# Windowed attention and a gated convolution on one core: second scores moved behind the values, on three single banks

## The chip, the cores and the metric

The kernel runs on one core of a Trainium2 chip. What counts is the device time of one execution in microseconds; the shown time is the median of three runs. The engines are TensorE (PE, with its weight loads as PEld), VectorE (DVE), ScalarE (ACT), GpSimd (POOL) and SyncE (SP), which issues the transfers. Each works through its own instructions in the order in which they were issued.

## The reference, cut to what matters

```python
# attention: q, k, v are [4, 8, 768, 64] fp32; n_sink = 4, window = 128
scores = q @ k.T / 8                       # per batch and head
keep   = (key < n_sink) | (0 <= query - key < window)
a = softmax(where(keep, scores, -1e9))     # denominator + 1e-9
x = a @ v                                  # then [4, 768, 512]
# gated convolution, d_model = 512, 5 taps, along the sequence
gate = sigmoid(causal_conv(x, conv_w))
out  = (gate * (x @ w_val)) @ w_out
```

Each query looks at 128 keys behind it and at the four sink keys; the first queries of a sequence have no keys of an earlier block.

## The kernel before

The work is cut into 24 *steps*: four batches, three blocks p of 256 rows, two groups qd of four heads. Two steps make a *module* of 256 rows by 512 channels. A step loads its q, k and v. `scores` (L343 on) is called twice, for two heads each (s0 and s1): eight small 64x64 fp32 matmuls (L356; the trace shows each as two) write 200 columns for each of two halves c and two heads j into `ss`, a tile of two PSUM banks that exists once. DVE then moves the diagonal block (copy_predicated, L361) and masks and takes the minimum of each half (L366). ACT takes exponentials (L374), DVE the reciprocal (`recip`, L379 and L380), POOL normalises (L388) and makes the sinks' shares. PE transposes the probabilities in two groups of four (L405, `probs_t`: tx and ty) into `tr`, a pool of two banks; `probs_x` on DVE (L427, L429) and `probs_y` on ACT (L436) spread them into the masked weights `wt`. PE transposes the sinks (L410), DVE masks them (L420). `values` (L453) makes xv from `wt` and v with 64x64 matmuls, `sinks` (L460) adds to it with 128-wide ones. ACT copies xv (`xt` L470, `xh` L474, and the four columns of the past, L478), POOL makes the low part `xl` (L484) and the last tap (L488), DVE the other four taps in eight instructions (L496), ACT the tanh (L501). A module then has four `val` calls (L515, 12 matmuls each; v0 to v3), `gated` on DVE (L526), its high part on ACT (L530) and its low part on POOL (L534), four `outp` calls (L545, 6 matmuls each; o0 to o3), and two stores (L549 on ACT, L551 the transfer). High and low parts take three passes of fp32r matmuls instead of one in fp32.

The order is written by hand: tables give each call of each step a time, in steps, and all calls are issued sorted by it. `WHEN` holds the general times, `EARLY` the exceptions of the first and last steps, `DECODE` those of the weights, which arrive as float64 bits and are decoded at the start (`_decode`; `bias` is L146 and L166). `FIRST` and `FILL` give idle matmuls at the start (`busy`, L219). The four calls on one bank line:

```python
ps_s = ctx.enter_context(tc.tile_pool(name="ps_s", bufs=1, space=PSUM))   # ss: one tile of two banks
ps_t = ctx.enter_context(tc.tile_pool(name="ps_t", bufs=2, space=PSUM))   # tr: two tiles of one bank
```

In `WHEN`, s0 is at -0.1928 and s1 at 0.3255, values at 1.8427, counted from the start of the own step; so s0 of a step stands just before the values of the step two earlier, and s1 about half a step behind them.

Of the kernel before, what the change touches and what calls it, by code (L numbers as in the profile page):

```python
# [19 lines left out]
DM = 512  # L20
# [14 lines left out]
WHEN = dict(kq=-1.9615, vv=-0.3611, s0=-0.1928, e0=0.4814, s1=0.3255, e1=0.5848, rec=0.6245, vl=1.4302, norm=0.667,  # L35
            tx=0.9562, ty=1.2383, sk=1.1919, ev=1.1901, yv=1.3942, ts=1.226, val=1.8427, si=1.874, xc=2.044,
            xh=2.2668, hd=2.0069, xl=2.2917, c4=2.0938, c0=2.2838, c1=2.5363, th=2.774, v0=0.4208, v1=0.4433,
            v2=0.7542, g0=0.6699, v3=0.8679, h0=0.7252, l0=1.0416, g1=0.9504, h1=1.0551, l1=1.282, o0=1.3729,
            o1=1.5265, o2=1.3969, t0=2.127, o3=2.081, t1=2.5321, cw=-67.148)

EARLY = {("kq", 0): -111.3041, ("vv", 0): -51.6322, ("s0", 0): -67.4875, ("e0", 0): -63.9472, ("s1", 0): -63.8218,
# [52 lines left out]
        ("scores", (3, 0)): 10}  # L94
SKA = 6

CUT = [("wo", 0), ("wo", 1), ("wo", 2), ("wo", 3)]
LAG = 3


# [30 lines left out]
def _decode(nc, pool, raw, n, whi, wlo, shape, unit=None, bank=None):  # L131
# [29 lines left out]
    def high():  # L161
        nc.scalar.activation(out=whi, in_=tf, func=AF.Copy)
# [635 lines left out]
```

## Time and profile before

| what | us |
|---|---|
| median of three runs | 282.35 |
| the three runs | 281.14, 282.35, 282.41 |
| the profiled execution, its time | 280.02 |
| its span, first to last instruction | 278.1 |
| PE busy | 264.1 |
| DVE busy | 221.5 |
| ACT busy | 180.8 |
| POOL busy | 175.6 |

The mean granted TensorE clock over the span was 0.993 of full speed. Busy times are sums over instructions that partly overlap, so an engine's share near 100% says that it hardly waited, and a pitch (start to start) says what one instruction costs the queue.

### The profile page before, as it was taken

How to read it: one execution, taken by the hardware profiler on the slowest of the kernel's cores; microseconds unless marked ns; L12 is line 12 of the kernel's file. 1: busy time of each engine (PE TensorE's matmuls, PEld its weight loads, DVE VectorE, ACT ScalarE, POOL GpSimd, SP SyncE). 2: the span in 40 equal slices, each digit the busy share in tenths (PEclk: the TensorE clock that was granted, in tenths of full speed). 3: DMA queues.
4: the chain of work that ended last, by engine and by line, in shares of the span. 5: the costliest groups of instructions: out<-in, count | busy, mean ns of one | idle time of the engine just before them, and what ended most of it. 6: DMA issues, size and time to landing. Idle time of an engine off the chain costs nothing.

```text
span 278.1 us, 8153 instructions
## 1 busy us (share of the span) xinstructions
PE 264.1 (95%) x2981; PEld 215.1 (77%) x2984; DVE 221.5 (80%) x827; ACT 180.8 (65%) x605; POOL 175.6 (63%) x226
## 2 busy tenths in 40 slices
PE   8897699999999999999999999999999999999991
PEld 3444369679789789789788888888888798798880
DVE  5999999988977986986986896896887898877510
ACT  3799967846865874774785685675676668564421
POOL 3378976974875675566667748648658729647330
PEclk9999999999999999999999999999999999999997
DMA  6993960047516417318317326336236232010202
GB/s 198 328 377 123 354 192 13 1 144 247 154 42 202 147 40 242 106 42 245 106 44 245 100 87 204 101 113 180 96 116 202 76 128 59 11 67 2 75 5 85
DMA packets 27391, 36.87 MB, mean 133 GB/s; under 512 B 2256, under 2 KB 23760, under 8 KB 27344
## 3 DMA queue, kind: packets, MB, share of 16 engines
q1 hardware_dynamic: 27344, 36.27, 40.1%
q8 instruction: 26, 0.43, 0.6%
q14 instruction: 21, 0.17, 0.2%
HBM read 29.97 MB, written 6.29 MB: 130 GB/s over the span
## 4 chain that ended last, share of the span: by engine, by line
PE 77%; POOL 8%; DVE 6%; ACT 5%; issue 2%; POOLq 0%; ACTq 0%
PE acc L515 23%; PE acc L545 21%; PE ss L356 11%; PE xv L453 10%; PE tr L405 6%; PE acc L219 3%; PE xv L460 3%; POOL wx L388 2%; DVE sg L496 2%; ACT w L374 2%; DVE sx L366 1%; POOL sg L488 1%; ACT xt L470 1%; POOL xl L484 1%; POOL wol L178 1%
## 5 line engine op out<-in xcount | busy, mean ns | idle before, releaser
L388 POOL TENSOR_TENSOR wx<-w,sm 128x512 f32<-128x512 f32 x48 | 49.3, 1047 | 60.2 <-DVE sm L380 45.2
L496 DVE SCALAR_TENSOR_TENSOR sg<-xv,cw,sg 128x256 f32<-128x256 f32 x192 | 78.9, 475 | 5.8 <-POOL sg L488 5.8
L374 ACT ACTIVATE w<-sx,ngm 128x132 f32<-128x132 f32 x192 | 75.1, 398 | 4.1 <-DVE ngm L366 4.1
L515 PE MATMUL acc<-xh,wvh 128*128 128x256 f32 x192 | 49.3, 291 | 0.3 <-ACT xh L474 0.3
L515 PE MATMUL acc<-xh,wvl 128*128 128x256 f32 x192 | 47.1, 280 | 0.0
L366 DVE CUSTOM_DVE_ANT_0 sx<-ss,mask 128x132 f32<-128x132 f32 x192 | 45.2, 292 | 1.6
L356 PE MATMUL ss<-k,q 64*64 64x200 f32 x768 | 43.6, 342 | 1.7 <-DVE ngm L366 0.8
L545 PE MATMUL acc<-woh,gh 128*128 128x512 f32 x96 | 39.9, 416 | 0.0
L515 PEld LDWEIGHTS acc<-xh,wvh 128*128 128x128 f32 x192 | 36.0, 188 | 3.9 <-DVE sg L496 2.3
L545 PE MATMUL acc<-woh,gl 128*128 128x512 f32 x96 | 38.1, 397 | 0.0
L545 PE MATMUL acc<-wol,gh 128*128 128x512 f32 x96 | 38.0, 396 | 0.1
L374 ACT ACTIVATION_READ_ACCUMULATOR w<-sx,ngm 128x1 f32 x192 | 37.1, 193 | 0.0
L515 PEld LDWEIGHTS acc<-xh,wvl 128*128 128x128 f32 x192 | 36.2, 189 | 0.0
L356 PEld LDWEIGHTS ss<-k,q 64*64 64x64 f32 x768 | 24.9, 132 | 14.3 <-issue 8.7
L534 POOL TENSOR_TENSOR gl<-sg,gh 128x512 fp32r<-128x512 f32 x24 | 31.5, 1313 | 5.7 <-ACT gh L530 5.7
L453 PEld LDWEIGHTS xv<-wt,v 64*64 64x64 f32 x1024 | 32.2, 133 | 3.4 <-ACT wt L436 0.9
L453 PE MATMUL xv<-wt,v 64*64 64x192 f32 (+2 forms) x1024 | 33.5, 274 | 0.4 <-ACT wt L436 0.4
L484 POOL TENSOR_TENSOR xl<-xt,xh 128x512 fp32r<-128x512 f32 x24 | 30.9, 1288 | 1.7 <-ACT xh L474 1.7
L515 PE MATMUL acc<-xl,wvh 128*128 128x256 f32 x192 | 30.8, 281 | 0.9 <-POOL xl L484 0.9
L488 POOL TENSOR_TENSOR sg<-xt,cw 128x512 f32<-128x512 f32 x24 | 25.2, 1051 | 10.2 <-ACT xt L470 10.1
L405 PE MATMUL tr<-ident,wx 128*128 128x128 f32 x192 | 28.2, 274 | 0.0
L361 DVE COPY_PREDICATED ss<-low,ss 128x256 f32<-128x256 uint8 x48 | 20.3, 424 | 9.2 <-PE ss L356 9.0
(108 smaller groups left out, 426.5 us busy)
## 6 DMA issues: line engine op xcount, KB each, us to landing
k<-in_kt_dram SPq DMA_DIRECT2D x23, 408.0 KB, 4.1
v<-in_vt_dram SPq DMA_DIRECT2D x16, 384.0 KB, 3.4
out_dram<-osb SPq DMA_DIRECT2D x24, 256.0 KB, 2.1
q<-in_qt_dram SPq DMA_DIRECT2D x23, 256.0 KB, 4.3
raw<-in_w_val_dram SPq DMA_DIRECT2D x4, 512.0 KB, 6.1
v<-in_vt_dram SPq DMA_DIRECT2D x8, 256.0 KB, 3.6
raw<-in_w_out_dram SPq DMA_DIRECT2D x4, 512.0 KB, 6.1
vs<-in_vsk_dram SPq DMA_DIRECT2D x8, 128.0 KB, 3.5
```

The costliest lines, as they stand in the source:

```text
L356: nc.tensor.matmul(ss[e * D:(e + 1) * D, j, c * n:(c + 1) * n], q[js, g, (2 * c + e) * D:(2 * c + e + 1) * D], k[js, g, (2 * c + e) * HB:( ...
L366: nc.vector.tensor_tensor_reduce(out=sx[:, j, c], in0=sv[:, j, c, :PK], in1=mask[:, c if p == 0 else 2], op0=ALU.add, op1=ALU.min, scale=- ...
L374: nc.scalar.activation(out=w[:, g, j, c], in_=sx[:, j, c], func=AF.Exp, scale=-1.0, bias=ngm[:, g, j, c:c + 1], accum_out=sm[:, g, j, c:c ...
L388: nc.gpsimd.tensor_tensor(out=t[:, n].rearrange("p c h x -> p h c x"), in0=w[:, :, :, at], in1=sm.to_broadcast([P, 4, 2, D]), op=ALU.mult)
L405: nc.tensor.transpose(out=x[:, o:o + P], identity=ident, in_=ws[s][:, n, c, 2 * g:2 * g + 2].rearrange("p j x -> p (j x)"))
L453: nc.tensor.matmul(acc[o * D:(o + 1) * D, g, x0 + h * D:x0 + (h + a1 - a0 + 1) * D], v[js, g, n], t[js, g, n, a0:a1 + 1].rearrange("p a r ...
L484: nc.gpsimd.tensor_tensor(out=xl[:, g], in0=xts[s], in1=xh[:, g].bitcast(F32), op=ALU.subtract)
L488: nc.gpsimd.tensor_tensor(out=sg[s // 2][:, g], in0=xts[s], op=ALU.mult, in1=cw[:, g, KT - 1:].to_broadcast([P, 2, PQ]))
L496: nc.vector.scalar_tensor_tensor(out=g, in0=x, scalar=a, in1=g, op0=ALU.mult, op1=ALU.add)
L515: nc.tensor.matmul(acc[:, h], a[:, kc, cs], x[:, kc], start=(n == 0), stop=(n == 11))
L534: nc.gpsimd.tensor_tensor(out=gl, in0=g, in1=gh.bitcast(F32), op=ALU.subtract)
L545: nc.tensor.matmul(acc, a[:, kc, ts], x[:, kc], start=(kc + n == 0), stop=(kc + n == 5))
```

## The change: what it does

1. `ps_s` holds three tiles of one bank. A call of `scores` takes two of them, one per head, in turn; copy_predicated is issued once per head instead of once per call. `ps_t` has one bank.
2. s1's time in `WHEN` goes from 0.3255 to -0.1247. On PE it then stands right behind the values, before the sinks.
3. For p == 0 and half c == 0, 132 score columns instead of 200 are computed, copy_predicated works on half c == 1 alone, and two mask entries swap places. `probs_x` there is two multiplications on half the columns and a copy; `probs_y` is two instructions.
4. The addition of 1e-9 in `recip` goes from DVE to POOL. The bits of the convolution's weights are decoded together with one piece of w_val. `bias` of w_out goes from ACT to POOL.
5. For the last module, `xl` and `gl` are made on DVE instead of POOL. Its last `outp` is computed in two column halves, and its last store copies one half on ACT and one on DVE and sends two transfers.
6. All other times in the tables are new too; `FIRST` is 24 instead of 16, and `FILL` 6, 4, 3, 4, 10 instead of 6, 5, 7, 4, 10 at other places.

```diff
-WHEN = dict(kq=-1.9615, vv=-0.3611, s0=-0.1928, e0=0.4814, s1=0.3255, e1=0.5848, rec=0.6245, vl=1.4302, norm=0.667,
+WHEN = dict(kq=-1.9648, vv=-0.3087, s0=-0.1933, e0=0.6676, s1=-0.1247, e1=0.51, rec=0.7342, vl=0.4618, norm=1.1365,
...
-FIRST = 16
+FIRST = 24
...
+        if cut:
+            nc.gpsimd.tensor_scalar(out=pf, in0=hi.bitcast(F32), scalar1=2.0 ** -112, scalar2=None, op0=ALU.mult)
+        else:
+            nc.scalar.activation(out=pf, in_=hi.bitcast(F32), func=AF.Copy, scale=2.0 ** -112)
...
-    ps_s = ctx.enter_context(tc.tile_pool(name="ps_s", bufs=1, space=PSUM))
+    ps_s = ctx.enter_context(tc.tile_pool(name="ps_s", bufs=3, space=PSUM))
-    ps_t = ctx.enter_context(tc.tile_pool(name="ps_t", bufs=2, space=PSUM))
+    ps_t = ctx.enter_context(tc.tile_pool(name="ps_t", bufs=1, space=PSUM))
...
-        ss = ps_s.tile([P, 2, 512], F32, name="ss", tag="ss")
+        ss = [ps_s.tile([P, 512], F32, name="ss", tag="ss") for _ in range(2)]
         for c in range(2):
+            x0 = HB if p == 0 and c == 0 else 0
             for j in range(2):
                 for e in range(2):
-                    nc.tensor.matmul(ss[e * D:(e + 1) * D, j, c * n:(c + 1) * n],
+                    nc.tensor.matmul(ss[j][e * D:(e + 1) * D, c * n + x0:(c + 1) * n],
...
-        nc.vector.copy_predicated(sv[:, :, :, :D], low[:, None, None, :].to_broadcast([P, 2, 2, D]),
-                                  sv[:, :, :, 2 * HB:])
         for j in range(2):
+            cs = slice(1, 2) if p == 0 else slice(0, 2)
+            nc.vector.copy_predicated(sv[:, cs, :D], low[:, None, :].to_broadcast([P, cs.stop - cs.start, D]),
+                                      sv[:, cs, 2 * HB:])
...
-        nc.vector.tensor_scalar(out=sm, in0=sm, scalar1=1e-9, scalar2=None, op0=ALU.add)
+        nc.gpsimd.tensor_scalar(out=sm, in0=sm, scalar1=1e-9, scalar2=None, op0=ALU.add)
         nc.vector.reciprocal(out=sm, in_=sm)
...
+        for m, k, n in ((cur, 0, 2), (prev, 2, 0)):
+            nc.vector.tensor_tensor(out=t[:, :, h0 + n:4 + n, k], in0=x[:, :, h0:], ...
+        if h0:
+            nc.vector.tensor_copy(out=t[:, :, 2, 1], in_=x[:, :, 1])
...
+        (nc.vector if s // 2 == LAST else nc.gpsimd).tensor_tensor(out=xl[:, g], in0=xts[s], ...
+        (nc.vector if m == LAST else nc.gpsimd).tensor_tensor(out=gl, in0=g, ...
+        for cs in ((slice(0, DM // 2), slice(DM // 2, DM)) if (m, i, h) == (LAST, 1, 1) else (slice(0, DM),)):
...
+            if n == 0:
+                nc.scalar.activation(out=ob[:, cs], in_=x, func=AF.Copy, scale=0.5)
+            else:
+                nc.vector.tensor_scalar(out=ob[:, cs], in0=x, scalar1=0.5, scalar2=None, op0=ALU.mult)
+            nc.sync.dma_start(out=out[m // NP, at:at + P, cs], in_=ob[:, cs])
```

On PE, in the middle of the program, before: the first scores of a step (ss, eight matmuls of one form), the values (xv), the sinks, the first transposes (tr), an output call, and then sinks' and second transposes with the second scores behind them.

```order
L356 MATMUL ss<-k,q 64x200 x8
L453 MATMUL xv<-wt,v 64x192 x8
L453 MATMUL xv<-wt,v 64x128 x4
L453 MATMUL xv<-wt,v 64x64 x4
L460 MATMUL xv<-skt,vh 128x256 x2
L405 MATMUL tr<-ident,wx 128x128 x4
...
L410 MATMUL acc<-ident,skb_105 128x128
L405 MATMUL tr<-ident,wx 128x128 x4
L356 MATMUL ss<-k,q 64x200 x8
L515 MATMUL acc<-xh,wvh 128x256
```

The second scores stand here between two 128-wide kinds of work, transposes and the val calls. After the change PE has, at such a place (the scores are those of a step with p == 0, hence the 132):

```order
L356 MATMUL ss<-k,q 64x132 x4
L356 MATMUL ss<-k,q 64x200 x4
L462 MATMUL xv<-wt,v 64x64 x4
L462 MATMUL xv<-wt,v 64x128 x4
L462 MATMUL xv<-wt,v 64x192 x8
L462 MATMUL xv<-wt,v 64x128 x4
L462 MATMUL xv<-wt,v 64x64 x4
L356 MATMUL ss<-k,q 64x132 x4
L356 MATMUL ss<-k,q 64x200 x4
L469 MATMUL xv<-skt,vh 128x256 x2
L407 MATMUL tr<-ident,wx 128x128 x4
L412 MATMUL acc<-ident,skb_105 128x128
```

Both groups of scores and the values now stand as one stretch of 64x64 work, and the second transposes come later, behind an output and a val call.

On DVE, before, behind a call of `scores` and its gated product: the masked weights, the sinks, half the convolution, and only then the evaluation of the second scores.

```order
L526 SCALAR_TENSOR_TENSOR sg<-sg,acc 128x512
L427 TENSOR_TENSOR wt<-tr,cur 128x2x4x64
L429 TENSOR_TENSOR wt<-tr,prev 128x2x4x64
L420 TENSOR_TENSOR skt<-acc,blk 128x256
L496 SCALAR_TENSOR_TENSOR sg<-xv,cw,sg 128x256 x4
L361 COPY_PREDICATED ss<-low,ss 128x2x2x64
L366 ISA sx,ngm<-ss,mask 128x132
```

After, with the four heads of a step evaluated one behind the other (the last of them in the first rows), then sinks, masked weights and the convolution in one piece:

```order
L364 COPY_PREDICATED ss<-low,ss 128x2x64
L368 ISA sx,ngm<-ss,mask 128x132
L368 ISA ngm 128x1
...
L422 TENSOR_TENSOR skt<-acc,blk 128x256
L430 TENSOR_TENSOR wt<-tr,cur 128x2x4x64
L430 TENSOR_TENSOR wt<-tr,prev 128x2x4x64
L505 SCALAR_TENSOR_TENSOR sg<-xv,cw,sg 128x256 x8
L382 RECIPROCAL sm<-sm 128x8
L535 SCALAR_TENSOR_TENSOR sg<-sg,acc 128x512
```

The convolution has moved as a block behind the masked weights, and the addition ahead of the reciprocal is gone from DVE.

More of the change, by code (lines that the diff above doesn't have):

```diff
@@ L186, in total @@
         acc.append(a := bank())
-        nc.tensor.matmul(a, one, tf, start=True, stop=False)
+        nc.tensor.matmul(a, one, tf[:, :DM], start=True, stop=False)
         nc.tensor.matmul(a, minus, whi, start=False, stop=False)
-        nc.tensor.matmul(a, plus, f, start=False, stop=True)
+        nc.tensor.matmul(a, plus, f[:, :DM], start=False, stop=True)
     def low():
-        nc.scalar.activation(out=wlo, in_=acc[0].rearrange("p (k m) -> p k m", m=shape[-1]) if len(shape) == 3
-                             else acc[0], func=AF.Copy)
-    return (bias, bits, share, high) + ((add,) if unit is None else (rest, scaled) if cut else (total, low))
+        nc.scalar.activation(out=wlo, in_=wide(acc[0]), func=AF.Copy)
+    return (bias, bits, share, high) + ((rest, scaled) if cut else (total, low)) + ((tf[:, DM:], ff[:, DM:]),)
 def banded(ctx, tc, wts, cw, zero, ident, scalars, flag, qt, kt, vt, vsk, w_val, conv_w, w_out, out):
```

109 lines of the change are left out of this document (54 added, 55 removed), and 99 rows, old and new, of tables (DECODE, EARLY).

## The prediction

> **What bounds the kernel now.** I read the page's busy times first, then a table of windows over the span, then the timeline of PE and of DVE in one step of the steady part, and last the timelines of the start and the tail.
>
> ```profile
> PE 264.1 (95%) x2981; PEld 215.1 (77%) x2984; DVE 221.5 (80%) x827; ACT 180.8 (65%) x605; POOL 175.6 (63%) x226
> PE 77%; POOL 8%; DVE 6%; ACT 5%; issue 2%; POOLq 0%; ACTq 0%
> ```
>
> The second line is the chain that ended last, by engine. PE carries three quarters of it. Where it does not shows in the windows (PE, PEld, DVE, ACT, POOL busy, then granted clock, transfers):
>
> ```profile
> 0.00:41.00 41.00, 34.03 (x294) 18.53 (x297) 36.28 (x141) 31.73 (x104) 27.60 (x44) 1.00 0.77 260
> 41.00:62.00 21.00, 20.35 (x247) 16.58 (x248) 19.38 (x62) 14.86 (x45) 15.84 (x19) 1.00 0.17 54
> 62.00:262.00 200.00, 199.44 (x2382) 171.14 (x2380) 162.52 (x620) 131.19 (x454) 129.53 (x163) 1.00 0.38 121
> 262.00:272.40 10.40, 10.25 (x62) 8.82 (x62) 3.28 (x7) 2.57 (x5) 2.58 (x2) 1.00 0.07 25
> 272.40:278.10 5.70, 0.00 (x0) 0.00 (x0) 0.00 (x0) 0.49 (x1) 0.00 (x0) 0.68 0.28 97
> ```
>
> From 62 to 262 us PE is busy for 199.44 of 200 us at full clock, while DVE has 37 us free, ACT 69, POOL 70. There only fewer or cheaper PE instructions save time, as long as no other engine makes PE wait. The first 41 us are the weights' decoding and the first step's chain; the last 5.7 the last store.
>
> **Part 1: the second scores join the values.** What one group costs PE is read from start to start. One step:
>
> ```profile
> 110.92 0.60 PE L405 MATMUL tr<-ident,wx 128*128 128x128 f32 x4
> 111.45 0.91 PE L356 MATMUL ss<-k,q 64*64 64x200 f32 x16
> 112.29 0.50 PE L545 MATMUL acc<-woh,gh 128*128 128x512 f32 x1
> 112.63 0.39 PE L545 MATMUL acc<-wol,gh 128*128 128x512 f32 x1
> ...
> 116.36 0.40 PE L545 MATMUL acc<-woh,gl 128*128 128x512 f32 x1
> 116.68 0.91 PE L356 MATMUL ss<-k,q 64*64 64x200 f32 x16
> 117.41 1.50 PE L453 MATMUL xv<-wt,v 64*64 64x64 f32 x48
> 118.84 0.50 PE L460 MATMUL xv<-skt,vh 128*128 128x256 f32 x2
> 119.18 0.60 PE L405 MATMUL tr<-ident,wx 128*128 128x128 f32 x4
> 119.53 0.47 PE L545 MATMUL acc<-woh,gh 128*128 128x512 f32 x1
> 119.84 0.39 PE L545 MATMUL acc<-wol,gh 128*128 128x512 f32 x1
> ```
>
> The same 16 score records take 0.84 us (111.45 to 112.29) when 128-wide work follows and 0.73 (116.68 to 117.41) when the 64x64 values follow. Four transposes take 0.53 ahead of scores (110.92 to 111.45) and 0.35 ahead of an output call (119.18 to 119.53). The first output matmul takes 0.34 behind scores (112.29 to 112.63) and 0.31 behind transposes. So a lone second call costs 0.53 + 0.84 + 0.34 - 0.35 - 0.31 = 1.05. Behind the values it enters from its own kind and leaves in the values' place: 0.73. Each joined call saves 0.32. Steps 6 to 23, 18 calls, lie in the steady part (those before stand in the start, counted below): 18 x 0.32 = **-5.8 us**. The saving is PE's own time, not a wait, so nothing needs to be late next for it to count; it is lost only where another engine then paces.
>
> **Part 2: the narrow scores.** A call is four groups of 200 columns in 0.73, so 0.18 a group and 0.0009 us a column. Two groups lose 68 columns: 2 x 68 x 0.0009 = 0.12. Steps 6, 7, 12, 13, 18, 19 have two such calls: 12 x 0.12 = **-1.5**. The four of steps 0 and 1 are in the start and taken at nothing; there the chain of weights and probabilities sets the time.
>
> **Part 3: what DVE gets.** Its rows in the same step, and two groups by form:
>
> ```profile
> 111.02 0.68 DVE L427 TENSOR_TENSOR wt<-tr,cur 128x512 f32<-128x512 f32 x1
> 112.22 0.41 DVE L420 TENSOR_TENSOR skt<-acc,blk 128x256 fp32r<-128x256 f32 x1
> 114.18 0.42 DVE L361 COPY_PREDICATED ss<-low,ss 128x256 f32<-128x256 uint8 x1
> 114.63 0.30 DVE L366 CUSTOM_DVE_ANT_0 sx<-ss,mask 128x132 f32<-128x132 f32 x1
> 115.50 1.66 DVE L496 SCALAR_TENSOR_TENSOR sg<-xv,cw,sg 128x256 f32<-128x256 f32 x4
> ...
> L429 DVE TENSOR_TENSOR wt<-tr,prev 128x256 f32<-128x256 f32 x8 | 3.3, 414 | 0.0
> L269 DVE CAST mk<-mk 128x64 f32<-128x64 int32 x1 | 0.2, 195 | 0.8 <-POOL mk L268 0.8
> ```
>
> A call's four reductions take 0.87 (114.63 to 115.50), so 0.43 a head; copy_predicated ahead of them takes 0.45 with its hand-over. Split by heads it is two instructions of 128 columns, for which there is no row: between 0.20 (64 columns, L269) and 0.42 (256 columns, L361). I take 0.31, the middle, since 128 columns lie between the two. A call then takes 2 x (0.31 + 0.43) = 1.48 instead of 1.32, a step 0.3 more (from nothing to 0.5). The split masked weights for p == 0 are two of 0.41 and a copy of at most that, 1.2 at most, as the two of L427 and L429 took (111.02 to 112.22). All this lies in DVE's free 37 us: 18 steps x 0.3 = 5.4. The cover is time within the step, too. From the start of the first scores DVE needs half a call, 0.37, then four heads, 2.5 to 3.4, then the sinks 0.41 and the weights 1.2: it frees the transposes' bank 4.5 to 5.4 after. PE in that time does scores 0.73, values 1.43, scores 0.73, sinks 0.34, transposes 0.35, and, as the new order has it, an output and a val call of about 1.4 each (six matmuls at 0.23, 112.63 to 116.36 being 16 of them; the val call taken alike): 6.4. The single bank therefore costs nothing while DVE starts these less than 1 us late. The first bank given back to the second scores is likewise wanted 0.73 + 1.43 + 0.18 = 2.3 after the start, and DVE has read it by 0.37 + 0.9 = 1.3. Taken at nothing; without the cover it is the first and the third rival.
>
> **Part 4: work moved to POOL.** The 24 additions and four `bias` go to an engine with 70 us free. Their price there varies:
>
> ```profile
> 35.55 0.83 POOL L394 TENSOR_SCALAR skb<-skb 128x32 fp32r<-128x32 f32 x1
> 59.00 0.29 POOL L394 TENSOR_SCALAR skb<-skb 128x32 fp32r<-128x32 f32 x1
> L405 PEld LDWEIGHTS tr<-ident,wx 128*128 128x128 f32 x192 | 22.1, 141 | 1.2 <-issue 0.6 <-POOL wx L388 0.3
> ```
>
> The same small instruction takes 0.29 or 0.83. The addition now stands on the chain from exponentials over reciprocal and normalising to the transposes, so it delays that chain by 0.1 to 0.6 against a like one on DVE (0.20, L269). PE waited for the normalised probabilities 0.3 us in all, so they came in time, and the second scores now start 0.45 of a step earlier, which gives the chain some 4 us more (a step is about ten: 61.65 to 272.4 us is ten and a half modules). Taken at nothing, bounded by 0 and, if the cover were gone in each of 18 steps, 18 x 0.5 = 9. The Trainium skill, "SBUF — State Buffer", in its terms (shared port pair), says that DVE and GpSimd share a pair of ports that one instruction holds to its end while the other engine waits. By that rule the 0.83 is waiting for DVE; the trace shows the stretched row but not its cause, and by the rule a busier POOL would pay it more often, which is the fourth rival.
>
> **Part 5: the tail.**
>
> ```profile
> 259.63 1.04 POOL L488 TENSOR_TENSOR sg<-xt,cw 128x512 f32<-128x512 f32 x1 [3.54 <-ACT xt L470]
> 260.63 1.28 POOL L484 TENSOR_TENSOR xl<-xt,xh 128x512 fp32r<-128x512 f32 x1
> 261.97 0.50 PE L515 MATMUL acc<-xl,wvh 128*128 128x256 f32 x2 [0.48 <-POOL xl L484]
> 272.29 0.60 ACT L549 ACTIVATE osb<-acc 128x512 f32<-128x512 f32 x1 [0.80 <-PE acc L545]
> out_dram<-osb SPq DMA_DIRECT2D x24, 256.0 KB, 2.1
> ```
>
> PE waits 0.48 for `xl`, which stands behind the last tap on POOL. On DVE it takes 0.68 (the row of L427) beside POOL: -0.48. The last store is 0.60 on ACT and then a transfer of median 2.1; two halves of it end at 0.41 (256 columns on DVE), and half a transfer saves from nothing to 1. I take -0.3 for both. The last output in two halves has the same columns in twice the instructions: nothing. Together **-0.8**, from -0.5 to -1.7.
>
> **Part 6: the start.** Here all tables are new, and I followed the new order by hand with durations of the rows.
>
> ```profile
> 4.57 2.00 PE L219 MATMUL acc<-zero 128*128 128x512 bf16 x8
> 25.15 1.10 PE L453 MATMUL xv<-wt,v 64*64 64x192 f32 x24 [0.37 <-ACT wt L436]
> 41.11 0.50 PE L515 MATMUL acc<-xl,wvh 128*128 128x256 f32 x2 [0.39 <-POOL xl L484]
> 49.88 0.91 PE L356 MATMUL ss<-k,q 64*64 64x200 f32 x16 [0.48 <-DVE ngm L366]
> 51.72 0.58 ACT L474 ACTIVATE xh<-xv 128x512 fp32r<-128x512 f32 x1
> 61.65 0.39 PE L515 MATMUL acc<-xh,wvh 128*128 128x256 f32 x1
> ```
>
> Eight more idle matmuls cost 8 x 0.24 (2.00 for eight, L219) = 1.9 ahead of the first scores, beside the transfers of the weights; earlier loads win it back: the first values come at about 22.8 instead of 25.15. The first val call ends its waiting at 41.9 to 42.5 instead of 41.11. The second module's first val call stood at 61.65. If nothing waits in between it comes at about 61.9. But in step 2 two of DVE's conv instructions now precede ACT's `xh`, which reads the same bank and waits for them; behind it on ACT queue the first module's second gated part, the sinks and exponentials of the next steps. Then `xh` (51.72 before) starts near 56, POOL's `gl` ends near 58, PE's first outputs wait about 3.5 us, and the val call comes near 65.8. So the start costs between +0.3 and +4.2; I take **+2.5**, nearer the upper end, since that wait is in the order and only its length is my estimate. Below nothing: if the 2.3 us that the first values gain were kept, -2.3.
>
> **The sum.** -5.8 - 1.5 - 0.8 + 2.5 = -5.6 against the profiled execution's 280.02 (1.92 around its span): 274.4. That execution is 2.33 under the median of 282.35, so I add 2.33: **276.7**. About 1.4 us, 0.5%, is what a measurement of this kernel can tell from no change.
>
> **The rivals.**
> First, DVE paces: it is at 81% from 62 to 262, and a step of ten us shrinks to about 9.6. With heads at 0.42 it has 8.1 + 0.5 in 9.6, and one long block of eight conv instructions stands ahead of the values' bank. If a wait of 0.32 per step takes the place of part 1: 276.7 + 5.8 = 282.5 with the start at +2.5, 280.3 with it at +0.3. Against it: the covers of 1 us in part 3.
> Second, the start gains: the first values' 2.3 us are kept, and 276.7 - 2.5 - 2.3 = 271.9. For it: fewer `FILL` matmuls and an earlier step 0. Against it: `xl` of step 1 still sets the first val call, not earlier than 41.9.
> Third, slower: the one transposes bank. The second transposes wait for the masked weights. If DVE reaches these more than 1 us late, each further microsecond is PE's; at 1.4 us late 0.4 a step, 18 x 0.4 = 7.2, so 283.9; from 1.3 us late (18 x 0.3 = 5.4) it eats the gain. For it: DVE's late row here would be `gated`, which waits for PE. Against it: 37 us free.
> Fourth, the additions on POOL are stretched as at 35.55 and the chain is late: 18 x 0.5 = 9 at most, 285.7; it decides when the chain loses its 4 us, which nothing in the rows suggests.
> Fifth, the lone call costs no more than a joined one, because PE's ends are modelled and its waits hidden: only parts 2, 5, 6 are left, 282.5. Against it: the starts, which repeat in every step.
>
> **How the numbers follow.** My forecast, PE still bound, start from +0.3 to +4.2: 274.5 to 278.4 by the start alone; chance 0.60. DVE pacing 0.15 (about 279.5 to 282.5), the start gaining 0.12 (270 to 273.5), one bank 0.06, POOL 0.03, no gain from joining 0.04. The range 271.5 to 281.5 leaves out some of the second rival below and the third, fourth and part of the first and fifth above, near 2 in 10. Faster by over 0.5% (under 280.9): 0.60 + 0.12 + half of the first rival, 0.80. Within 0.5%: the rest of the first and the fifth, 0.11. Slower: 0.09.
>
> **What would show it.** Part 1: second scores directly behind the values at about 0.73 to the next start in the steady part, and second transposes at 0.35 to 0.45. Part 2: 0.61 for a narrow call. Two steady steps together 0.6 to 0.9 us shorter. Part 3: no wait of PE for DVE at scores or second transposes over 0.2; else a rival. Part 5: no wait at `xl` of the last step. Part 6: the second module's first val call between 62 and 66. The prediction is wrong if PE's waits between 62 us and the tail add up to more than 3 us, or if the second module starts outside those bounds.

## The result: 294.6 us, 4.7% slower

The median of the changed kernel is 294.6 us (four runs, 294.04 to 295.78) against 281.75 for the kernel before beside it: a ratio of 1.0469, interval 1.0412 to 1.0527. The prediction was 276.7, in 271.5 to 281.5, with a chance of 0.09 for slower. It was wrong, by 17.9 us. The two profiled executions differ by 14.5 us and not by the medians' 12.9, because that of before (280.02) lies 1.7 under its median; all that is read from the two traces below holds for these two.

The profile after, by busy times and the chain that ended last:

```profile
PE 267.9 (92%) x2991; PEld 219.8 (75%) x2993; DVE 230.8 (79%) x861; ACT 178.1 (61%) x606; POOL 182.2 (62%) x247
PE 67%; POOL 11%; DVE 10%; ACT 8%; issue 2%; POOLq 0%; DVEq 0%; ACTq 0%
```

PE's share of the chain fell from 77% to 67%: something else now sets the end for a tenth more of the span. Windows say where (PE, PEld, DVE, ACT, POOL busy, granted clock, transfers), first the ones shown of before, the last two moved to the new end:

```profile
0.00:41.00 41.00, 33.00 (x277) 17.58 (x279) 35.80 (x136) 27.85 (x91) 28.41 (x42) 0.96 0.71 242
41.00:62.00 21.00, 15.25 (x159) 12.88 (x154) 19.61 (x53) 8.65 (x23) 15.17 (x18) 0.92 0.23 71
62.00:262.00 200.00, 196.08 (x2340) 168.83 (x2341) 160.57 (x636) 132.57 (x475) 131.34 (x180) 0.99 0.40 121
262.00:287.00 25.00, 23.56 (x224) 20.50 (x223) 14.77 (x36) 9.04 (x18) 7.33 (x9) 1.00 0.09 33
287.00:292.70 5.70, 0.00 (x0) 0.00 (x0) 0.00 (x0) 0.00 (x0) 0.00 (x0) 0.65 0.19 58
```

From 41 to 62 us PE is busy for 15.25 instead of 20.35. The steady part is as full as it was. Cut at each module's first val call, the span of 292.7 against 278.1 (+14.6) divides so:

| from, to | before | after | difference | predicted |
|---|---|---|---|---|
| start to the second module's first val call | 61.65 | 74.76 | +13.1 | +2.5 |
| eight modules in the middle (third to eleventh) | 161.31 | 161.70 | +0.4 | about -6.5 |
| the modules before and behind these | 48.90 | 49.02 | +0.1 | about -1.3 |
| last PE start to the end | 6.2 | 7.2 | +1.0 | -0.3 |

The middle, before and then after, each in one window from first val call to first val call:

```profile
82.27:243.58 161.31, 161.23 (x1936) 137.87 (x1932) 133.75 (x521) 106.85 (x378) 104.69 (x135) 1.00 0.40 125
```

```profile
95.45:257.15 161.70, 160.77 (x1937) 138.69 (x1936) 134.06 (x533) 105.86 (x379) 109.75 (x151) 1.00 0.41 124
```

PE is busy nearly throughout in both, at full clock. One group of four transposes falls behind the window of before (124 of them instead of 128), which is the +0.4; the first seven modules, alike in number of matmuls, take 141.02 and 141.22. So the joined scores gained nothing although PE stayed the bound, and the start lost nearly everything. These are two questions, with the store as a third.

### The profile page after: what moved, and what is told of

Read it like the earlier page. It is cut to its first block, busy times and chain, and to the rows that moved or that the text cites. A ratio compares the mean times of both kernels' runs of the same rounds, so it can differ in the third digit from the quotient of the medians.

```text
span 292.7 us, 8212 instructions
## 1 busy us (share of the span) xinstructions
PE 267.9 (92%) x2991; PEld 219.8 (75%) x2993; DVE 230.8 (79%) x861; ACT 178.1 (61%) x606; POOL 182.2 (62%) x247
## 4 chain that ended last, share of the span: by engine, by line
PE 67%; POOL 11%; DVE 10%; ACT 8%; issue 2%; POOLq 0%; DVEq 0%; ACTq 0%
PE acc L524 23%; PE acc L556 19%; PE ss L356 9%; PE xv L462 8%; PE tr L407 4%; POOL wx L390 4%; ACT w L376 3%; DVE sx L368 2%; PE xv L469 2%; DVE sg L505 2%; POOL xl L493 1%; DVE sg L535 1%; PE acc L224 1%; DVE ss L364 1%; POOL vh L258 1%
## 5 line engine op out<-in xcount | busy, mean ns | idle before, releaser
L368 DVE CUSTOM_DVE_ANT_0 sx<-ss,mask 128x132 f32<-128x132 f32 x192 | 49.1, 293 | 3.4
L556 PE MATMUL acc<-woh,gh 128*128 128x512 f32 (+1 forms) x98 | 41.6, 424 | 5.0 <-ACT skt L420 4.4
L356 PE MATMUL ss<-k,q 64*64 64x200 f32 (+1 forms) x768 | 43.5, 328 | 2.0 <-DVE ss L364 1.3
L479 ACT ACTIVATE xt<-xv 128x512 f32<-128x512 f32 x24 | 14.3, 597 | 50.0 <-PE xv L469 49.8
L364 DVE COPY_PREDICATED ss<-low,ss 128x128 f32<-128x128 uint8 (+1 forms) x96 | 26.0, 271 | 21.0 <-PE ss L356 20.4
L556 PE MATMUL acc<-woh,gl 128*128 128x512 f32 (+1 forms) x98 | 39.0, 398 | 0.0
L556 PE MATMUL acc<-wol,gh 128*128 128x512 f32 (+1 forms) x98 | 38.7, 395 | 0.0
L524 PE MATMUL acc<-xl,wvh 128*128 128x256 f32 x192 | 32.8, 291 | 2.8 <-POOL xl L493 2.8
L543 POOL TENSOR_TENSOR gl<-sg,gh 128x512 fp32r<-128x512 f32 x22 | 28.3, 1288 | 10.2 <-ACT gh L539 10.2
L524 PEld LDWEIGHTS acc<-xl,wvh 128*128 128x128 f32 x192 | 27.4, 193 | 3.7 <-POOL xl L493 3.0
```

Source lines behind the costliest of these rows:

```text
L356: nc.tensor.matmul(ss[j][e * D:(e + 1) * D, c * n + x0:(c + 1) * n], q[js, g, (2 * c + e) * D:(2 * c + e + 1) * D], k[js, g, (2 * c + e) * ...
L364: nc.vector.copy_predicated(sv[:, cs, :D], low[:, None, :].to_broadcast([P, cs.stop - cs.start, D]), sv[:, cs, 2 * HB:])
L368: nc.vector.tensor_tensor_reduce(out=sx[:, j, c], in0=sv[:, c, x0:x0 + PK], in1=mask[:, c if p == 0 else 2], op0=ALU.add, op1=ALU.min, sca ...
L479: nc.scalar.activation(out=t, in_=accs[s][:, :, KT - 1:KT - 1 + PQ], func=AF.Copy)
L524: nc.tensor.matmul(acc[:, h], a[:, kc, cs], x[:, kc], start=(n == 0), stop=(n == 11))
L543: (nc.vector if m == LAST else nc.gpsimd).tensor_tensor(out=gl, in0=g, in1=gh.bitcast(F32), op=ALU.subtract)
```

## The start: a read order, seen and sized too small

The timelines of ACT, DVE and PE after, at the place that part 6 named:

```profile
60.31 1.65 DVE L505 SCALAR_TENSOR_TENSOR sg<-xv,cw,sg 128x256 f32<-128x256 f32 x4
...
62.05 0.60 ACT L483 ACTIVATE xh<-xv 128x512 fp32r<-128x512 f32 x1 [4.94 <-DVE sg L505]
62.55 0.62 ACT L539 ACTIVATE gh<-sg 128x512 fp32r<-128x512 f32 x1
63.07 0.62 ACT L420 ACTIVATE skt<-acc,blk 128x128 fp32r<-128x128 f32 x2
...
63.74 0.79 PE L556 MATMUL acc<-woh,gh 128*128 128x512 f32 x1 [4.36 <-ACT skt L420]
64.33 0.63 PE L556 MATMUL acc<-wol,gh 128*128 128x512 f32 x1
```

ACT stands for 4.94 us at `xh` until DVE's four conv instructions, which read the same bank and come first in the order, are done at 61.96. The gated part and the sinks queue behind it, and PE waits 4.36. The first experiment puts `xh` of step 2 back ahead of those taps. Each experiment was timed beside runs of the kernel before (medians 280.83 to 282.95); its ratio is to these.

**Experiment 1.** The changed kernel, one time in the table:

```diff
-         ("xh", 2): 2.3232,
+         ("xh", 2): 2.3050,
```

> The changed kernel with one number of its table changed: in step 2 the copy xh stands ahead of DVE's first conv taps instead of behind them; every engine's own order stays. Theory A (the start fails at this read order): xh starts near 57 instead of 62.05 us, the first outputs lose their 4.4 us wait and the half clock behind it, and the time falls by 4 to 6.5 us, to about 288.5 to 290.5. Rival B (the exponentials and the reciprocal of step 4, or POOL, are as late anyway): less than 1 us.

Measured 288.98, ratio 1.0275 (1.0229 to 1.0322): 5.6 us less than the change.

```profile
57.08 0.60 ACT L483 ACTIVATE xh<-xv 128x512 fp32r<-128x512 f32 x1
```

`xh` starts at 57.08, not 62.05, and the second module's val call comes at 68.64 instead of 74.76. This cause is shown. It leaves 7.0 us of lateness against 61.65.

**Experiment 4.** `bias` of w_out back on ACT (POOL took 1550 ns for each, ahead of an `xl`, where ACT takes 0.68 us):

```diff
-        if cut:
+        if False:
```

> The changed kernel with the bias of w_out back on ACT. Theory A (POOL's 1.5 us bias stands directly ahead of xl of step 1, so the first val call waits for it and then runs at half clock): the first val call goes on 1.5 us earlier or more, and the time falls by 1.5 to 4 us. Rival B (what follows waits for DVE's conv and the second copy anyway): less than 1 us.

Measured 294.77, 1.0467 (1.042 to 1.0513): no change. What it may be worth appears only once step 2 is mended (experiment 13 below).

**Experiment 5.** A stretch of PE at half the granted clock follows the wait for `xl` at 46.5. Does that stretch cost time? Experiment 1 and eleven idle matmuls inside the wait:

```diff
+            if (m, u, h, n) == (0, 0, 0, 10):
+                busy(11)
```

> The kernel of the first experiment (xh of step 2 ahead of the conv) with eleven idle matmuls in the wait of the first val call for xl of step 1; nothing waits for them but PE. Theory A (after a long idle stretch PE runs at half clock for some 3.4 us, so the wait costs about 1.7 us more than its own length): the granted clock of 46 to 50 us is near 1.0 and the time falls by 1.2 to 2 us from 288.98. Rival B (what follows is set by ACT and POOL, not by PE's clock): within 0.5 us.

Measured 288.99, 1.0267 (1.0223 to 1.0311): no change. The windows of experiment 1, then of this one:

```profile
46.00:48.00 2.00, 1.52 (x7) 1.52 (x8) 1.97 (x3) 1.10 (x4) 1.83 (x3) 0.59 0.00 0
```

```profile
46.00:48.00 2.00, 2.00 (x14) 1.40 (x12) 1.97 (x3) 1.08 (x6) 1.84 (x3) 1.00 0.13 46
...
40.00:44.00 4.00, 4.00 (x48) 3.88 (x40) 3.89 (x15) 2.76 (x11) 3.75 (x6) 0.59 0.22 54
```

The clock at 46 to 48 rose to 1.00, but in this execution another half-clock stretch stood at 40 to 44. It lies ahead of the idle matmuls (these start at 44.79), so they didn't bring it; the last section has another case of a stretch that one execution has and another hasn't. Nothing was gained in sum, so this run doesn't say what a start at full clock throughout would bring.

**Experiment 8.** The changed code with the old order of steps 0 to 5, of modules 0 and 1 and of the decoding, `bias` on ACT, and the old idle matmuls; second transposes of the first steps shifted so that they fit one bank:

```diff
-FIRST = 24
+FIRST = 16
...
-FILL = {("scores", (1, 1)): 6, ("decode_weights", ("wv", 2, 4)): 4, ("scores", (2, 1)): 3, ...
+FILL = {('scores', (0, 0)): 6, ('decode_weights', ('wv', 0, 4)): 5, ('scores', (1, 0)): 7, ...
```

> The changed kernel with the order of before for the start: steps 0 to 5, modules 0 and 1, the weights' decoding (bias on ACT) and the idle matmuls have before's times, and the second transposes are moved behind the masked weights there, as one bank wants; from step 6 on all is as changed. Theory A (the loss is the start's, the steady part is a draw): the first val call of the second module near 62 us, and 281 to 284 us in all. Rival B (the banks and the joined scores lose time themselves): over 287. My prediction's terms without the start: 274.

Measured 305.13, 1.0835 (1.0781 to 1.0889), far over what either theory gave. PE's timeline:

```profile
27.50 1.12 PE L351 MATMUL tr<-ident,wx 128*128 128x128 f32 x4 [4.97 <-DVE wt L378]
...
65.44 1.09 PE L351 MATMUL tr<-ident,wx 128*128 128x128 f32 x4 [6.33 <-DVE sm L326]
```

With one bank, transposes stand at the head of PE's queue until DVE has emptied it, 5.0 and 6.3 us here (the second releaser reads `sm`, the reciprocal, which ends 0.1 us behind the masked weights). The old order, shifted in this way, loses more with one bank than the new one does, so this run doesn't separate the two. Seven modules of its steady part take 141.7 us, in the changed kernel 141.6, before 141.5.

**Experiments 11, 13 to 16.** What else could the remaining 7 us be? All start from experiment 1: `xl` of step 1 ahead of POOL's `bias` (11); `bias` on ACT (13); that and the old times of w_out's decoding (14); without the ten idle matmuls at the sinks' transpose (15); 14 and 15 together (16).

```diff
(11)  ("wo", "a"): (-39.9423, -26.5964, 1.0375 -> 1.48, -2.645)
(13)  if cut:  ->  if False:
(14)  as 13, and the ("wo", ...) rows of DECODE as before
(15)  FILL without ("sinks_t", (1,)): 10
```

> The kernel of the first experiment (288.98 us) with xl of step 1 on POOL ahead of the third bias of w_out instead of behind it. Theory A (the chain from 45 us on starts at this xl): the first val call goes on 1.5 us earlier, and the time falls by 1 to 1.7 us. Rival B (DVE's decoding, which waits for the bias, is as late): within 0.5 us.

> The kernel of the first experiment (288.98 us) with the bias of w_out back on ACT. Theory A (POOL's biases, 1.5 us each, stand in the chain at 24 and 43.7 us, and the read order had hidden that in the fourth experiment): 1 to 3 us less. Rival B (the chain goes round them through ACT): within 0.7 us.

> As the last, and the decoding of w_out at the times of the kernel before, of which one piece lies behind the steps' start there instead of ahead of them. Theory A (the changed order decodes w_out too early, and DVE's and POOL's work for it delays the first modules): 2 to 5 us below the last. Rival B (the chain of probabilities is as late anyway): within 0.7 us; or slower, where the first outputs then wait for w_out.

> The kernel of the first experiment without the ten idle matmuls behind the sinks' transpose of step 1 (3.41 us at half clock, from 31.66 us, in its chain). Theory A (they hold up the transposes and scores behind them): 1.5 to 3.4 us less. Rival B (the clock is lowered in that place anyway and the chain goes through POOL): within 0.7 us.

> Bias on ACT, old decoding of w_out and no ten idle matmuls together, on the kernel of the first experiment. Theory A (these are what is left of the start's loss): 282.5 to 286. Rival B (the start is bound by the one bank for transposes and by the joined scores' order): over 287.

Measured 288.99 (11), 287.84 (13; 1.0215, 1.0133 to 1.0296), 291.41 (14), 288.87 (15) and 291.41 (16), against 288.98 of experiment 1. Only `bias` on ACT may give something: 1.1 us, but experiment 1's ratio of 1.0275 lies within its interval. The old times of the decoding cost 3.6 on top of it; idle matmuls are worth nothing.

**Experiment 17.** The trace of 13 shows the same order of reads a second time, in step 0: ACT's `xh` behind DVE's taps, eight exponentials behind it, and in the end PE at the scores of step 3.

```profile
36.89 0.60 ACT L483 ACTIVATE xh<-xv 128x512 fp32r<-128x512 f32 x1 [1.30 <-DVE sg L505]
...
40.48 0.72 PE L356 MATMUL ss<-k,q 64*64 64x200 f32 x10 [1.85 <-DVE ngm L368]
```

```diff
-         ("xh", 0): -3.562,
+         ("xh", 0): -5.5,
```

> The kernel with the copy of step 2 and the bias moved back (287.84 us), and with xh of step 0 as well moved ahead of the first half of its convolution and of eight exponentials. In that run ACT's xh of step 0 started at 36.89 (1.30 behind DVE's taps), the exponentials behind it ended at 38.9, POOL waited 2.72 for them, DVE took the reciprocal at 39.39, and PE waited 1.85 for scores at 40.48. Theory A (the same order of reads also sets the first module): xh starts at 33.9, the reciprocal at 38.2, and PE's wait is 0.7: 1.2 us less, 286.7. Rival B (the wait covers another, from the one bank of transposes or the decoding): 287.4 to 288.3, and PE waits as long at another place before the first val call.

Measured 286.69, 1.0174 (1.0114 to 1.0233): 1.15 less than 13, as the first theory had it. That it fits to a tenth of a microsecond is luck: 0.4% is within the intervals. The trace says more.

```profile
33.49 0.59 ACT L483 ACTIVATE xh<-xv 128x512 fp32r<-128x512 f32 x1
...
40.26 0.72 PE L356 MATMUL ss<-k,q 64*64 64x200 f32 x10 [0.70 <-DVE ngm L368]
```

`xh` now follows `xt`, and PE's wait is 0.70, as expected. The second module's val call comes at 66.42.

**Experiment 18.** 17, with step 0's convolution behind the evaluation of step 3's scores on DVE, and without four idle matmuls:

```diff
-         ("c0", 0): -4.2447, ("c1", 0): -2.8295,
+         ("c0", 0): -1.3, ("c1", 0): -1.2,
...
-FILL = {..., ("decode_weights", ("wv", 2, 4)): 4, ...}
+FILL = {..., ...}
```

> The kernel with the copy of step 2, the copy of step 0 and the bias moved back, and in addition both halves of step 0's convolution stand behind the evaluation of step 3's scores on DVE, and four idle matmuls ahead of step 0's second transposes are left out (PE waited 2.38 at them for ACT's copy of the weights, and the transposes came at 24.44). Theory A (order alone makes the first module late): transposes near 22.6, which takes up to 1.8, and DVE frees the scores' banks some 1.4 us earlier: 2.5 to 3.5 us less than the 287.84 it starts from, 284.3 to 285.3, and the first val call, at 44.26 there, comes near 41. Rival B (something these do not touch, such as the one transposes bank or the decoding): within 1 us of 287.84.

Measured 290.38, 1.031 (1.0246 to 1.0374): 3.7 slower than 17. The scores came 1.7 us earlier, as expected (38.55 instead of 40.26). But the values of step 1 write xv, which exists once, and so waited until DVE had read step 0's (DVE's convolution, and PE's values):

```profile
40.71 3.22 DVE L505 SCALAR_TENSOR_TENSOR sg<-xv,cw,sg 128x256 f32<-128x256 f32 x8
...
44.03 2.20 PE L462 MATMUL xv<-wt,v 64*64 64x192 f32 x32 [4.58 <-issue]
```

The releaser reads "issue", so the profile places no releaser here; the taps end at 43.9, and PE starts. The expectation had overlooked that reader. The transposes came at 24.06, not 22.6.

Of the 13.1 us, the traces give back 8.3 (74.76 to 66.42): 6.1 by `xh` of step 2, which is shown; 0.6 by `bias` and 1.6 by `xh` of step 0 (1.15 of it the shorter wait), both of a size by which executions with the same first steps differ too. **Open: 4.8 us**, the first steps in their new order. In the trace of 17 PE waits there 2.4 us for a copied weight (`wvl`) and 2.6 for the sinks' shares of POOL; whether one transposes bank forces these, or an order without them exists, no run decided. Some of the 4.8 may be the trace of before: by medians 17 is 4.3 slower than before in all (286.69 against 282.42, the store's loss included), by the traces 7.2. And experiment 10, which leaves the first steps in the order of before, has this val call at 64.76 in its trace instead of 61.65; the last section shows where the first of these 3.1 us arise.

## The steady part: three seams and a wait for one that was saved

From the starts of all PE instructions in the seven modules that are alike in number of matmuls, the mean time from the first start of a kind to the start of what follows, summed over a module (two steps):

| work in a module | before | after | difference |
|---|---|---|---|
| values | 2.57 | 2.35 | -0.22 |
| four groups of transposes | 1.85 | 1.66 | -0.19 |
| first scores | 1.46 | 1.39 | -0.06 |
| second scores | 1.68 | 1.74 | +0.06 |
| transposes of the sinks | 0.23 | 0.41 | +0.17 |
| val calls | 5.91 | 6.11 | +0.20 |
| output calls | 5.87 | 5.94 | +0.07 |
| sinks | 0.58 | 0.58 | 0.00 |

The sum is +0.03 (differences are taken before rounding). The prediction has 0.64 less for joining and 0.16 for the narrow scores. Of the 0.64, 0.28 are for the scores (0.84 less 0.73 and 0.34 less 0.31, in two steps) and 0.36 for the transposes (0.53 less 0.35, in two steps). What took them back shows in PE's timeline after, a step whose values are short (32 records), and then one with long ones (48):

```profile
160.92 0.91 PE L356 MATMUL ss<-k,q 64*64 64x200 f32 x16
161.65 1.16 PE L462 MATMUL xv<-wt,v 64*64 64x192 f32 x32
162.63 1.12 PE L356 MATMUL ss<-k,q 64*64 64x200 f32 x16
163.68 0.39 PE L524 MATMUL acc<-xh,wvh 128*128 128x256 f32 x1
...
165.45 0.60 PE L407 MATMUL tr<-ident,wx 128*128 128x128 f32 x4
165.89 0.27 PE L412 MATMUL acc<-ident,skb 128*128 128x128 f32 x1
166.23 0.50 PE L556 MATMUL acc<-woh,gh 128*128 128x512 f32 x1
...
169.13 0.60 PE L407 MATMUL tr<-ident,wx 128*128 128x128 f32 x4
169.49 0.48 PE L556 MATMUL acc<-woh,gh 128*128 128x512 f32 x1
```

```profile
181.84 1.50 PE L462 MATMUL xv<-wt,v 64*64 64x64 f32 x48
183.16 0.86 PE L356 MATMUL ss<-k,q 64*64 64x200 f32 x16
183.94 0.39 PE L524 MATMUL acc<-xh,wvh 128*128 128x256 f32 x1
```

Second scores take 0.78 behind long values (183.16 to 183.94), not 0.73, since 128-wide work follows them. The exit from 64x64 work is paid here now, and no longer by the values (1.43 before, 1.32 after). Values and second scores take 2.10 together, where they took 2.27 apart (1.43 and 0.84): this part of the saving is there. Behind short values the second scores take 1.05 (162.63 to 163.68): their second head needs the bank of the first scores' first head, and DVE gives that back late, as its rows at the same place and the group of all such copies show.

```profile
161.86 0.30 DVE L364 COPY_PREDICATED ss<-low,ss 128x128 f32<-128x128 uint8 x1 [1.45 <-PE ss L356]
162.63 0.29 DVE L364 COPY_PREDICATED ss<-low,ss 128x128 f32<-128x128 uint8 x1
...
L364 DVE COPY_PREDICATED ss<-low,ss 128x128 f32<-128x128 uint8 x64 | 18.8, 293 | 15.4 <-PE ss L356 14.9
```

DVE starts the first head 0.94 after PE's first scores (161.86 against 160.92), not 0.37: the matmuls of the two heads alternate, so half a call doesn't complete a head. It turns to the second head at 162.63, 1.71 after the scores' start, where part 3 had the first done by 1.3; and behind short values PE wants the bank at just that time, not at the 2.3 that part 3 worked out with long ones. Six of the fourteen second calls are such, which is 0.2 a module.

The lone second transposes (169.13) cost 0.36, as hoped, but split a run of output or val calls, which then pay another entry: +0.07 and +0.20 a module. Part of the latter is waiting for POOL's `xl`, since the val call ahead of the lone transposes takes 1.44 to 1.63. And the transposes of the sinks, which stood before other transposes, now stand before output calls: 0.34 here (165.89 to 166.23), 0.21 in the mean against 0.12, part of it a wait for POOL. That a change of the tiling mode (here from 64x64 to 128-wide work) drains TensorE is what the Trainium skill says in "TensorEngine Tiling (Array Packing)", Key Properties; the trace agrees, with about 0.1 us for each crossing (1.43 against 1.32 for the values). In sum, a module gains about 0.3 by the scores beside the values, 0.13 by the narrow scores and 0.19 by the transposes, and pays 0.2 for the late bank, 0.17 at the sinks' transposes and 0.27 in the val and output calls.

**Experiment 10** tests the seam alone: the kernel before, with the second transposes moved out from in front of the second scores.

```diff
-            tx=0.9562, ty=1.2383, ..., yv=1.3942
+            tx=0.9562, ty=1.56, ..., yv=1.72
```

> The kernel before, with its two banks for transposes, but with the second transposes of steps 6 to 21 moved from their place beside the first into the output and val calls, as the changed order has them; the second scores then follow the sinks' transpose. Theory A (a lone group of transposes costs its seams, as much as it saves ahead of the scores): 0 to 3 us slower than before. Rival B (my prediction's reading: transposes between output and val matmuls cost nothing of their own, and four transposes ahead of scores cost 0.53, elsewhere 0.35): 1.5 to 3 us faster.

Measured 282.12, 1.0019 (0.9989 to 1.0049), the kernel before 281.24: nothing, and seven modules take 141.10 us instead of 141.02. Moving lone transposes pays as much as it saves. In the same table, a module's transposes take 0.18 less, but the transposes of the sinks, which now stand directly ahead of the second scores, take 0.18 more (0.21 each instead of 0.12); the val calls take 0.09 more and the output calls 0.09 less. So the 0.18 that the prediction booked for a group (0.53 to 0.35) isn't there. The run is half of what the expectation says: one of a module's two groups came to stand ahead of the first scores, at 0.53 again, and only the other in a val call, at 0.36.

**Experiment 2** undoes only the move of the second scores:

```diff
-  s1=-0.1247    ("s1", 22): -0.0925
+  s1=0.3255     ("s1", 22): 0.2768
```

> The changed kernel with the second scores back at their old time in the table (0.3255) from step 6 on, all else as changed. Theory A (joining saves about 0.33 us a call, and what cancels it lies elsewhere): 18 calls lose it, 4 to 7 us more, 299 to 302. Rival B (a joined call gains nothing here because it waits for DVE to free its bank): within 1.5 us of 294.6, or less.

Measured 337.39, 1.1969 (1.1915 to 1.2023). Both theories missed: with one transposes bank, the order of all else as changed, PE waits for it when the second scores stand elsewhere. The waits of PE, from 95 to 300 us (in total, times, longest):

```profile
PE tr L407 <- DVE wt L430: 14.2, 5, 2.9
PE tr L407 <- DVE wt L434: 7.7, 3, 2.6
```

So here banks and order can't be judged one without the other, and this run tells nothing on the 0.32.

**Experiment 6** is part 2 alone, on the kernel before: narrow scores, masks and split weights.

```diff
-                    nc.tensor.matmul(ss[e * D:(e + 1) * D, j, c * n:(c + 1) * n],
+                    nc.tensor.matmul(ss[e * D:(e + 1) * D, j, c * n + x0:(c + 1) * n],
```

> The kernel before with part 2 alone: 132 score columns in a sequence's first block, with its masks and masked weights; banks, order and tables as before. Theory A (PE's own time there): 12 calls x 0.12 = 1.4 us less, 280.5 to 281.2. Rival B (the columns are hidden behind waits of DVE): within 0.5 us.

Measured 280.43, 0.9969 (0.9938 to 0.9999). Nine modules took 180.79 instead of 181.93: 1.1 less, where 1.5 was predicted for all. The narrow calls cost what the rows promised, 0.61 instead of 0.73. But the medians differ by 0.4 us only (280.43 and 280.83), which the second theory would allow as well and which is under the half percent that a measurement tells apart safely.

**Experiment 9.** Is DVE close to pacing? Experiment 1, with POOL's `xl` ahead of its last tap, so that the val call no longer waits for it:

```diff
-            xl=2.424
+            xl=2.295
```

> The kernel of the first experiment (288.98 us) with POOL making xl ahead of the last tap from step 6 on, instead of behind it. Theory A (in the steady part the val call waits 0.2 us a module for xl, part of what eats the joined scores' gain): the val call of twelve matmuls ahead of the second transposes takes 1.44 instead of 1.63 us and the time falls by 1.5 to 2 us. Rival B (DVE's conv, which waits for the last tap, then ends later and holds the next values back): no change, or slower by up to 2 us.

Measured 296.73, 1.0545 (1.0509 to 1.0581), 7.7 slower than experiment 1. The val call's wait is gone, but DVE now waits for the tap:

```profile
DVE sg L505 <- POOL sg L497: 16.5, 14, 1.7
```

That is 92 to 250 us; eight modules take 169.5. A POOL instruction of 1.3 us out of place costs about 1 us a module here. There is slack in DVE's share (134 of 162 us), not in its order: the first rival's mechanism, though the change itself doesn't trip it.

## The tail

Timelines after, of ACT and DVE, and the group of transfers:

```profile
284.35 0.60 ACT L566 ACTIVATE osb<-acc 128x512 f32<-128x512 f32 x1 [2.81 <-PE acc L556]
285.79 0.38 ACT L566 ACTIVATE osb<-acc 128x256 f32<-128x256 f32 x1 [0.84 <-PE acc L556]
286.21 0.42 DVE L568 TENSOR_SCALAR osb<-acc 128x256 f32<-128x256 f32 x1 [3.95 <-ACT osb L566]
out_dram<-osb SPq DMA_DIRECT2D x2, 128.0 KB, 2.8
```

The halves don't run side by side: DVE's starts when ACT's is done. Both read one bank and both write `osb`; which of the two sets the order, no run shows. And the two half transfers land after 2.8 us in the median, the whole ones after 2.1.

**Experiment 3** stores the last piece whole:

```diff
-        for cs in (... if (m, i, h) == (LAST, 1, 1) else (slice(0, DM),)):
+        for cs in (... if False else (slice(0, DM),)):
...
-        last = (m, i) == (LAST, 1)
+        last = False
```

> The changed kernel with the last output and the last store in one piece, as before. Theory A (the two halves are copied one behind the other, and two transfers land later than one): 0.5 to 1.2 us less, about 293.6. Rival B (my prediction's term, halves in parallel): 0.3 us more.

Measured 293.82, 1.0427 (1.0384 to 1.0471): 0.8 less, as the first theory had it; with intervals of half a percent this is near what can be told. The traces agree on the sign: from PE's end to the end of the program it is 5.86 to 6.74 us in the six kernels that store whole, before among them, and 6.75 to 8.25 in the fourteen with halves. Of the size they say little (6.74 in this run's, 6.95 in the change's).

**Experiments 7 and 12** try the other half of part 5 on experiment 6: the last `xl` and `gl` on DVE (7), the last `xl` alone (12).

```diff
(7)  (nc.vector if s // 2 == B * NP - 1 else nc.gpsimd)   for xl, and so for gl (m == B * NP - 1)
(12) (nc.vector if s == 2 * B * NP - 1 else nc.gpsimd)   for xl only
```

> As the last, and the last module's low parts xl and gl on DVE instead of POOL. Theory A: the last val call's 0.48 us wait goes, 0.4 to 0.6 us below the kernel with the narrow scores alone. Rival B: DVE's conv, now behind xl, ends later and the gate takes it back: no difference or slower.

> The kernel before with the narrow scores (0.4 to 1.2 us faster by itself) and only the last step's xl on DVE. Theory A (the wait for gl on DVE had eaten the gain of xl): 0.4 to 0.6 us below the kernel with the narrow scores alone. Rival B: the conv behind it ends later and gives it back, no difference.

Measured 280.24 (0.9985, 0.9955 to 1.0016) and 280.47 (0.9974, 0.9947 to 1.0001), experiment 6 at 280.43 and 0.9969. No gain in the order of before: the wait goes to the gated product's low part, first 7 and then 12:

```profile
266.60 0.50 PE L555 MATMUL acc<-woh,gl 128*128 128x512 f32 x1 [0.99 <-DVE gl L544]
```

```profile
266.04 0.50 PE L555 MATMUL acc<-woh,gl 128*128 128x512 f32 x1 [0.58 <-POOL gl L544]
```

In the changed kernel, whose last module has another order, PE waits for neither `xl` nor `gl`. From that module's first val call to PE's end it takes 11.7 us, where before took 12.1. So the -0.48 seems to be there; it wasn't tried apart.

## Why the prediction was wrong, point by point

- **Part 6, +2.5, measured +13.1: the main failure.** The read order at `xh` was right and named at the right instruction, but its size was off: `xh` was put near 56 and PE's wait at 3.5; they were 62.05 and 4.36, and undoing the order gave 6.1 at the second module (experiment 1). The other 7.0 aren't in the prediction. Its hand-made timeline has "the first val call ends its waiting at 41.9 to 42.5"; it was 46.5. The first values did come early (23.8 instead of 25.15; it had 22.8). What was lost lies behind them: the first val call began 3.0 late (41.81 instead of 38.80) and then waited 2.75 for `xl`. The prediction looked for the order of reads in step 2 only; step 0 has the same (experiment 17). The upper bound of 4.2 was no bound: it took one wait, where everything ahead of it could be late too. The cause of 4.8 us stays open.
- **Part 1, -5.8, measured about nothing.** The failing step is "0.53 + 0.84 + 0.34 - 0.35 - 0.31", and in it the 0.53 - 0.35. It compared transposes ahead of scores with transposes ahead of output calls, as if the second group then had no cost of its own; its new place in the middle of an output or val run was counted at the price of a pair, and what now stands ahead of scores or output calls in its stead, the sinks' transposes, at nothing. These pay 0.17 more a module, the split runs 0.27. Experiment 10 shows the sum of this to be zero, for the half that it tries. The scores' own share was right in size (2.27 to 2.10 behind long values), and 0.2 a module of it went to the late bank of part 3.
- **Part 3, taken at nothing.** Nearly: no wait of PE for DVE at the second transposes in the middle. But the first head's bank comes late in six of fourteen calls, 0.3 each, by the wrong 0.37 and the long values. The 0.31 for copy_predicated was 0.293.
- **Part 2, -1.5.** About right in the traces (-1.1 by experiment 6); the medians can't tell it.
- **Part 4, nothing.** Right for the additions (0.242 us each on POOL, and no wait of PE behind them in the middle). `bias` costs at most the 1.1 of experiment 13.
- **Part 5, -0.8.** The store's -0.3 was a loss, 0.8 by experiment 3, as the two copies don't overlap. The -0.48 at `xl` came true as far as the trace shows, though in the order of before it moves to the next wait (7, 12).
- **The rivals.** The fifth, no gain from joining, was given 0.04 and came nearest in the middle, for another reason than it said. None had a start beyond +4.2, though with every table new the start was the least known term.

## What to carry to other kernels

A saving read from one seam is to be summed over the whole cycle of seams, with the moved work's new neighbours on both sides. Where an order is new throughout, look at every place where two engines read one PSUM bank: at `xh` the order of issue was the order of reading, and a queue stood behind the second reader. A bound on a start that was followed by hand has to take in that all behind one wait is late, and that a bank less (here for the transposes) can make an old order unusable.

## What the hardware showed that I had not expected

Behind pauses of PE the granted clock was about half for 3.4 us. Two windows after: a pause, and the stretch behind it:

```profile
43.90:46.40 2.50, 0.00 (x0) 0.00 (x0) 1.68 (x2) 2.50 (x11) 2.50 (x2) 1.00 0.77 282
46.50:49.90 3.40, 3.38 (x16) 3.39 (x17) 3.25 (x6) 0.83 (x3) 1.75 (x2) 0.51 0.00 0
```

The same stood behind the wait of 4.36 (0.53 from 63.7 to 67.1), where output matmuls came every 0.43 us instead of 0.23. In the trace of before, no window up to 62 us is under 1.00. But the clock falls in other executions of the same first steps. Before and then experiment 10, both behind a wait of 1.9 us of PE for `wvl`:

```profile
33.50:37.00 3.50, 3.45 (x45) 2.19 (x44) 3.35 (x15) 1.18 (x4) 3.33 (x5) 1.00 0.63 235
```

```profile
33.50:37.00 3.50, 3.28 (x8) 1.18 (x9) 3.35 (x15) 1.43 (x4) 3.33 (x5) 0.51 0.67 249
```

The eight idle matmuls there come every 0.43 us instead of 0.22, and PE is 1.7 us later behind them. A trace of one execution thus has a term that its order doesn't set.

By the Trainium skill, "TensorE: Matmul & The Clock Gate", Part 1, the clock halves after an idle window of some 3.4 us and comes back after about 3.4 us of work. The trace agrees on the half and on the way back; here a pause of 2.5 us was enough, in a start with other short waits ahead of it, and one of 1.9 us in one execution and not in another. About 1.2 of experiment 1's 5.6 us are of this kind (5.6 less the wait of 4.4), which is worked out and not tried apart.
